# An attention stage on one core: the global keys' product cut into four 64x64 tiles, and the copy of the transposed weights shared by two engines

## The chip, the core and the metric

The kernel runs on one core of a Trainium2 chip. The metric is the device time of one execution in microseconds; lower is better. A core has five engines that each take their own instructions in order: PE (TensorE, matrix products and transposes), DVE (VectorE), ACT (ScalarE), POOL (GpSimd) and SP (SyncE, which issues most DMAs). Engines wait for each other through semaphores. PE writes its results to PSUM, eight banks of 128 partitions by 512 float32; the other engines copy them from there to SBUF.

## The reference, cut to what matters

Attention over 4 x 8 heads with 512 local tokens and 32 global tokens of 64 numbers, followed by two dense blocks on the result (the second and third part of the kernel; the change does not touch them).

```python
s_ll = scale * q_l @ k_l.T; s_ll = where(|pos_i - pos_j| <= 32, s_ll, -1e9)
s_lg = scale * q_l @ k_g.T
a_l = softmax(concat([s_lg, s_ll]))
out_l = a_l @ concat([v_g, v_l])
s_g = scale * q_g @ concat([k_g, k_l]).T
out_g = softmax(s_g) @ concat([v_g, v_l])
x = concat([out_g, out_l])
```

A local query thus has two products with values: with the 32 global values, which all queries share, and with the values of its own window.

## The kernel before, in words

**Tiles and units.** `body` works on one pair of heads at a time: `p` runs over 16 pairs (`NP`). A pair's 512 queries are cut in two halves `u`, each of 256 queries, which are four windows of 64 queries. One (p, u) is the unit of the stage; a pass of the loop over `p` (line 930) holds two units' worth of every step, and "half A" below is its first, "half B" its second.

**Steps of a unit.** `scores` (lines 732 to 740) makes the products of queries and keys as 64x64 tiles: eight matrix products of 160 columns into two PSUM banks `s`; float32 takes two passes, so 16 instructions. `maxima` (742) is DVE's: per 128x160 tile it adds the mask, writes the sum to SBUF and takes the maximum. `exps` (751) is ACT's, with the sums as a by-product. `sums` and `norm` (758, 761) make the reciprocal on DVE and scale the four tiles on POOL. `transp` (779) transposes them on PE into bank `tc0` (four 128x128, the window keys) and `tc1` (one 128x128, the global keys). `transp_evac` (786) copies both to SBUF: ACT the 128x512 of `tc0` (line 788, to `p1`), DVE the 128x128 of `tc1` (line 790, to `p2`). `pv` (792) makes the products with the values: `glob` (806, two products of 128x128 weights with the 128 columns of `p2`) and `win` (799, eight products of 128x64 weights with 96 or 64 columns). Unit u writes PSUM bank `pv_ps[u]`. `pv_local` (825) and `pv_global` (831) copy that bank to `x` on DVE.

**Order.** The schedule is written by hand: each engine gets its instructions in the order of the loop body. In a pass p, PE does `scores(p,0)`, `transp(p-1,0)`, `pv(p-2,1)`, on odd p the global queries' scores `g_scores` (853), `scores(p,1)`, on even p the global queries' transposes `g_transp` (882), `transp(p-1,1)`, `pv(p-1,0)`. DVE does the maxima of (p,0), the reciprocal of (p-1,1), `pv_global(p-2,0)`, the `p2` copy of (p-1,0), on odd p three operations on the global queries (856 to 862), the maxima of (p,1), `pv_local` and `pv_global` of (p-2,1), the `p2` copy of (p-1,1). ACT does per half: two `exps`, the 128x512 copy, two `exps`; on even p two copies of `g_transp` (885, 886) stand ahead of the copy of half B.

**Other work in the same loop.** In passes 10 to 13 DVE has at the end of half B one 128x512 subtraction each (`x_low`, 216). In passes 8, 14, 16 and 17 it converts pieces of weights (`w_float`, 155, in three steps `step(0)` to `step(2)`, and a cast, 180). Passes 16 and 17 have no scores: `mm1` (224) of the first dense block stands in their place.

Of the kernel before, what the change touches and what calls it, by code (L numbers as in the profile page):

```python
# [22 lines left out]
DM, DFF = 512, 2048  # L23
# [58 lines left out]
def body(ctx, tc, qT, kW, v, w1i, w1o, w2i, w2o, coef, out):  # L82
# [50 lines left out]
    pv_ps = [ps.tile([128, 512], F32, name=f"pv{j}") for j in range(2)]  # L133
# [573 lines left out]
    p1_r = Ring("p1", ATT2 + 2 * VC + 2560, 640, 3, 2, 320)  # L707
# [24 lines left out]
    def scores(p, u):  # L732
        for i in range(2):
            for j in range(2):
                for a in range(2):
                    r, w = slice(64 * j, 64 * j + 64), 4 * u + 2 * i + (a if i else 1 - a)
# [35 lines left out]
    def g_copies(p, u):  # L772
        p1 = pT[p, u][0]
        a = pgT[p // 2][0]
        o = 64 * (p % 2)
        pool.tensor_copy(p1[:, :, 128:192].rearrange("p j (s c) -> p j s c", s=2),
                         a[:, 2 * u:2 * u + 2, o:o + 64].rearrange("p s (j c) -> p j s c", j=2))
# [14 lines left out]
    def pv(p, u):  # L792

        v = vt[p // 2]
        c = pgT[p // 2][1]
        p1, p2 = pT.pop((p, u))
        bank = pv_ps[u]

        def win(w, o0, o1, stop=False):
            for j in range(2):  # L800
                jj = 2 * (p % 2) + j
                pe.matmul(bank[64 * j:64 * j + 64, o0:o1], v[:, VW * w + 64 * jj:VW * w + 64 * jj + 64],  # L802
                          p1[:, j, o0 + (32 if o0 >= 128 else 0):o1 + (32 if o0 >= 128 else 0)],
                          start=False, stop=stop, skip_group_check=True)
# [7 lines left out]
        glob(0)  # L812
        glob(1)
        win(4 * u, 64, 160)
        win(4 * u + 1, 0, 64)
        win(4 * u + 2, 128, 224)
        win(4 * u + 3, 224, 288, stop=u == 0)
        if u:
            for j in range(2):
                jj = 2 * (p % 2) + j  # L820
                o = VE + 64 * jj
                pe.matmul(bank[64 * j:64 * j + 64, 128:160], v[:, o:o + 64], c[:, 32 * jj:32 * jj + 32],
                          start=False, stop=True, skip_group_check=True)

    def pv_local(p, half):
# [665 lines left out]
```

## Time and profile before

| | us |
|---|---|
| three runs | 843.36, 843.52, 844.43 |
| median | 843.52 |
| profiled execution, first to last instruction (span) | 841.8 |
| attention loop in the profile, first scores to the first product of pass 17 | 4.4 to 114.7 |
| PE busy over the span | 831.1 (99%) |
| DVE, ACT, POOL busy over the span | 707.4, 620.1, 187.2 |

The page gives no time for the profiled execution other than its span; the median of the runs is 1.7 us above the span, which is what lies around the instructions. TensorE's granted clock is at its upper level in all 40 slices of the page, and no run stands out. In the timeline view a row is one instruction or several alike that follow each other: start in us from the span's start, time it took, engine, line, operation, tiles, count, and in brackets idle time of the engine ahead of it. The time that an instruction took includes its way through the engine, so the next may start before it ends; what an instruction costs its engine is the distance from its start to the next start.

### The profile page before, as it was taken

What the parts mean: (1) busy time and instruction counts of PE and PEld (TensorE: products, weight loads), DVE (VectorE), ACT (ScalarE), POOL (GpSimd) and SP (SyncE); (2) the same over time, 40 slices, a digit from 0 to 9 for tenths busy, and PEclk for the clock granted to TensorE, in tenths of its full rate; (3) what the DMA queues carried; (4) which work ended last, traced back from release to release, by engine and by line L of the source; (5) the groups of instructions that cost most, each with busy time, mean ns of one, the idle gap of its engine ahead of it and who ended that gap; (6) DMA issues with size and microseconds to landing.
All of it is one profiled execution on the core that took longest, in us unless ns stands there. A gap on an engine that the chain in (4) does not pass through costs nothing.

```text
span 841.8 us, 15593 instructions
## 1 busy us (share of the span) xinstructions
PE 831.1 (99%) x5719; PEld 761.9 (91%) x5719; DVE 707.4 (84%) x1411; ACT 620.1 (74%) x1195; POOL 187.2 (22%) x352
## 2 busy tenths in 40 slices
PE   8999999999999999999999999999999999999997
PEld 4877788889999999999999999999899999898986
DVE  5687888994893597877968699999999999989997
ACT  6888867773453666767776797878897878888775
POOL 4666765660001111111111121111011011011100
PEclk9999999999999999999999999999999999999999
DMA  9686759922768899989987573433463443465401
GB/s 342 253 315 238 272 200 418 406 78 100 278 231 289 278 326 390 330 280 370 383 283 225 149 240 112 126 113 113 125 188 113 125 113 113 125 207 146 138 25 63
DMA packets 50540, 181.37 MB, mean 215 GB/s; under 512 B 5664, under 2 KB 8480, under 8 KB 49440
## 3 DMA queue, kind: packets, MB, share of 16 engines
q1 hardware_dynamic: 30976, 100.94, 32.0%
q0 software_dynamic: 18960, 79.18, 31.1%
q8 instruction: 45, 0.74, 0.4%
q10 hardware_dynamic: 528, 0.26, 0.1%
q14 instruction: 31, 0.25, 0.1%
HBM read 139.73 MB, written 40.63 MB: 214 GB/s over the span
## 4 chain that ended last, share of the span: by engine, by line
PE 84%; DVE 11%; ACT 2%; POOL 2%; issue 1%; ACTq 0%; POOLq 0%
PE s L404 27%; PE s L431 10%; PE pv L431 10%; PE tc L431 10%; PE s L233 9%; PE tc L243 5%; PE pv L243 5%; PE pv L802 2%; PE tc L783 2%; POOL sm L766 2%; PE s L738 1%; PE pv L808 1%; DVE g L496 1%; DVE x L516 1%; DVE x L520 1%; DVE e L512 1%
## 5 line engine op out<-in xcount | busy, mean ns | idle before, releaser
L404 PE MATMUL s<-sh,got 128*128 128x320 f32 (+1 forms) x1120 | 287.8, 320 | 0.8 <-DVE x L592 0.6
L404 PEld LDWEIGHTS s<-sh,got 128*128 128x128 f32 x1120 | 198.6, 188 | 2.9 <-DVE x L592 1.0
L396 POOL DMA_DIRECT2D got<-pr x120 | 64.7, 539 | 539.8 <-PE s L404 464.6
L404 PE MATMUL s<-sl,got 128*128 128x320 f32 (+1 forms) x560 | 179.1, 320 | 0.0
L431 PEld LDWEIGHTS s<-g,w 128*128 128x128 f32 x768 | 124.7, 188 | 10.9
L431 PE MATMUL s<-g,w 128*128 128x256 f32 x768 | 131.7, 280 | 0.0
L404 PEld LDWEIGHTS s<-sl,got 128*128 128x128 f32 x560 | 105.4, 188 | 0.9
L431 PE MATMUL tc<-g,w 128*128 128x384 f32 (+1 forms) x384 | 99.3, 366 | 0.2 <-DVE g L496 0.2
L431 PE MATMUL pv<-g,w 128*128 128x384 f32 (+1 forms) x384 | 99.1, 366 | 0.0
L233 PE MATMUL s<-xh,w 128*128 128x512 f32 (+1 forms) x256 | 76.8, 363 | 0.0
L492 ACT ACTIVATE g<-x 128x640 fp32r<-128x640 f32 (+1 forms) x79 | 61.4, 777 | 14.8 <-DVE x L537 13.1
L496 DVE TENSOR_TENSOR g<-x,g 128x640 fp32r<-128x640 f32 (+1 forms) x79 | 69.0, 874 | 1.0 <-ACT g L492 0.9
L431 PEld LDWEIGHTS tc<-g,w 128*128 128x128 f32 x384 | 65.2, 188 | 3.5 <-DVE g L496 0.8
L431 PEld LDWEIGHTS pv<-g,w 128*128 128x128 f32 x384 | 65.1, 188 | 2.8
L755 ACT ACTIVATE sm<-sm,nm 128x160 f32<-128x160 f32 x128 | 55.6, 441 | 9.3 <-DVE nm L747 9.0
L766 POOL TENSOR_SCALAR sm<-sm,rs 128x160 f32<-128x160 f32 x128 | 54.2, 449 | 34.3 <-DVE x L836 16.1
L512 DVE SCALAR_TENSOR_TENSOR e<-e,nf,e 128x768 f32<-128x768 f32 (+1 forms) x48 | 46.6, 971 | 10.4 <-ACT e L504 10.4
L233 PEld LDWEIGHTS s<-xh,w 128*128 128x128 f32 x256 | 47.3, 188 | 5.1
L747 DVE CUSTOM_DVE_ANT_0 sm<-s,mask 128x160 f32<-128x160 f32 x128 | 36.2, 321 | 15.7 <-PE s L738 8.9
L188 POOL TENSOR_TENSOR w<-cv,w 128x512 fp32r<-128x512 f32 x32 | 42.1, 1318 | 30.9 <-ACT w L182 23.1
L617 ACT ACTIVATE u<-s 128x320 f32<-128x320 f32 (+1 forms) x40 | 18.3, 457 | 41.4 <-PE s L404 41.4
L508 ACT ACTIVATE x<-x,nf 128x768 f32<-128x768 f32 (+1 forms) x48 | 47.1, 981 | 0.0
(192 smaller groups left out, 1748.3 us busy)
## 6 DMA issues: line engine op xcount, KB each, us to landing
got<-pr POOLq DMA_DIRECT2D x80, 512.0 KB, 4.1
got<-pr POOLq DMA_DIRECT2D x40, 768.0 KB, 4.8
pr<-half SPq DMA_DIRECT2D x24, 512.0 KB, 6.9
v<-in_v_dram SPq DMA_DIRECT2D x8, 1408.0 KB, 8.2
k<-in_kW_dram SPq DMA_DIRECT2D x15, 592.0 KB, 5.8
r<-in_w1i_dram SPq DMA_DIRECT2D x16, 512.0 KB, 9.8
r<-in_w1o_dram SPq DMA_DIRECT2D x16, 512.0 KB, 10.6
pr<-tw SPq DMA_DIRECT2D x16, 512.0 KB, 3.2
```

What stands on the lines that cost most here:

```text
L188: pool.tensor_tensor(w[:, 1], f, w[:, 0].bitcast(F32), op=ALU.subtract)
L233: pe.matmul(ph, w[:, half, 128 * kk:128 * kk + 128], b[:, kk, :n], start=(half == kk == 0 and b is hi), stop=(half == 1 and kk == KD - 1))
L243: pe.matmul(acc_bank[d][:, :n], w[:, half, 128 * d:128 * d + 128], src[:, :n], start=start, stop=stop)
L396: pool.dma_start(got[q % 2][:, o0:o1], pairs[q >= Q2][q % NPAIR][:, o0:o1])
L404: pe.matmul(bank(q, i), a[:, k], b[:, k], start=first and k == 0 and j == 0, stop=k == 1 and j == 2, skip_group_check=True)
L431: pe.matmul(dst, a, b, start=first and j == 0, stop=j == KF - 1 and final, skip_group_check=True)
L492: act.activation(gpair(q, f)[0], strip(q, 2 + f), AF.Copy)
L496: eng.tensor_tensor(gl, strip(q, 2 + f), gh.bitcast(F32), op=ALU.subtract)
L508: act.activation(t, h, AF.Identity, scale=nf[:, 3:4], bias=nf[:, 2:3])
L512: dve.scalar_tensor_tensor(a, in0=a, scalar=nf[:, 5:6], in1=b, op0=ALU.mult, op1=ALU.add)
L755: act.activation(e, e, AF.Exp, scale=-1.0, bias=nm[:, k:k + 1], accum_out=tot[:, k:k + 1])
L766: pool.tensor_scalar(e, e, rs[:, k:k + 1], 1.0, op0=ALU.mult, op1=ALU.mult)
```

## The change

The 128x128 products with the global values become four products of 64x64 weights (`common`), which write two banks: the first two windows of a unit go with bank 0 and the other two with bank 1, for both units, so that one bank now holds columns of both units and `pv_local` and `pv_global` read both banks. `pv` is split into `windows` and `common`, and `common` stands directly ahead of the next `scores` on PE. The copy of `tc0` is halved: ACT copies the first head's 256 columns, DVE the second's. `pv_local(p-2,0)` moves ahead of the maxima of (p,0), `pv_local(p-2,1)` and both parts of `pv_global` ahead of the maxima of (p,1). The order of the windows in the output and the layout of `p1` follow.

```diff
-    pv_ps = [ps.tile([128, 512], F32, name=f"pv{j}") for j in range(2)]
+    pv_two = ps.tile([128, 1024], F32, name="pv")
+    pv_ps = [pv_two[:, 512 * j:512 * j + 512] for j in range(2)]
...
     def transp_evac(p, u):
         p1, p2 = pT[p, u]
-        act.copy(bass.AP(tensor=p1.tensor, offset=p1.offset, ap=[p1.ap[0], [320, 2], [192, 2], [1, 128]]),
-                 tc_ps[0].rearrange("p (a b c) -> p a b c", a=2, b=2))
+        o = 32 if u else 0
+        for j, copy in enumerate((act.copy, dve.tensor_copy)):
+            copy(p1[:, j, :, o:o + 128], tc_ps[0][:, 256 * j:256 * j + 256].rearrange("p (i c) -> p i c", i=2))
         dve.tensor_copy(p2, tc_ps[1][:, 0:128])
...
-        def glob(i):
-            o = VG + 256 * (p % 2) + 128 * i
-            pe.matmul(bank[:, 160 * i:160 * i + 128], v[:, o:o + 128], p2, start=i == 0, stop=False,
-                      skip_group_check=True)
...
+    def windows(p, u):
+        v, p1 = vt[p // 2], pT[p, u][0]
+        for i in range(2):
+            w = 4 * u + 2 * i
+            for w, o, c, n in ((w, 0, 128, 96), (w + 1, 96, 224, 64)) if u else ((w, 64, 64, 96), (w + 1, 0, 0, 64)):
+                for j in range(2):
+                    jj = 2 * (p % 2) + j
+                    pe.matmul(pv_ps[i][64 * j:64 * j + 64, c:c + n], v[:, VW * w + 64 * jj:VW * w + 64 * jj + 64],
+                              p1[:, j, i, o:o + n], start=u == w % 2 == 0, stop=False, skip_group_check=True)
...
+    def common(p, u):
+        v, p2 = vt[p // 2], pT.pop((p, u))[1]
+        for i in range(2):
+            for j in range(2):
+                r, o = slice(64 * i, 64 * i + 64), VG + 256 * (p % 2) + 128 * i + 64 * j
+                pe.matmul(pv_ps[i][64 * j:64 * j + 64, 160 * u:160 * u + 128], v[r, o:o + 64], p2[r],
+                          start=False, stop=True, skip_group_check=True, tile_position=(64 * i, 64 * j))
...
                 scores(p, 0)
-                maxima(p, 0, 0)
-                exps(p, 0, 0)
             else:
                 mm1(p - NP)
             if 2 <= p:
                 pv_local(p - 2, 0)
+            if cur:
+                maxima(p, 0, 0)
+                exps(p, 0, 0)
...
             if 2 <= p:
-                pv(p - 2, 1)
+                windows(p - 2, 1)
             if odd and p > 1:
                 g_scores(g)
+            if 2 <= p:
+                common(p - 2, 1)
             if cur:
...
+            if 2 <= p:
+                pv_local(p - 2, 1)
+                pv_global(p - 2)
+            if cur:
                 maxima(p, 1, 0)
...
-            if 2 <= p:
-                pv_local(p - 2, 1)
-                pv_global(p - 2, 1)
             if pre:
                 transp(p - 1, 1)
...
             if pre:
-                pv(p - 1, 0)
+                windows(p - 1, 0)
+                common(p - 1, 0)
```

How the instructions stand on the engines, in the order of each engine; names in brackets are the semaphores that the instruction waits for, numbers behind names are buffers (`sm` the score tiles, `p_1` and the like `p1` and `p2`, `tc_182` is `tc0`).

DVE before, half A of a pass with even p, from the reciprocal of (p-1,1) to the first maximum of (p,1):

```order
L763 RECIPROCAL rs_417<-rs_417 128x4 [waits DVE_49]
L836 COPY x_62<-pv_184 128x32
L790 COPY p_1_403<-tc_183 128x128 [waits PE_49]
L747 ISA sm_425,nm_407<-s_180,mask_402 128x160 [waits PE_49,Pool_49]
```

The same place now:

```order
L764 RECIPROCAL rs_416<-rs_416 128x4 [waits DVE_49]
L791 COPY p_1_427<-tc_182 128x2x128 [waits Activation_49]
L792 COPY p_1_402<-tc_183 128x128 [waits PE_49]
L821 COPY x_62<-pv 128x256 [waits PE_49]
L827 COPY x_62<-pv 128x32
L828 TENSOR_TENSOR x_62<-x_62,pv 128x32 [waits DVE_49]
L748 ISA sm_424,nm_406<-s_180,mask_401 128x160 [waits PE_49,Pool_49]
```

Between the reciprocal and the maximum, DVE now has its half of the `tc0` copy, which waits for ACT, and the copies of the values' products of (p-2,1), which stood behind the maxima before.

PE before, from the transposes of a half B to the next scores:

```order
L783 MATMUL tc_182<-ident_401,sm_425 128x128 [waits Activation_49,Pool_49]
L783 MATMUL tc_182<-ident_401,sm_425 128x128 [waits Pool_49] x3
L784 MATMUL tc_183<-ident_401,sm_425 128x128 [waits DVE_49]
L808 MATMUL pv_184<-p_2_404,v_423 128x128 [waits DMAHW6_49]
L808 MATMUL pv_184<-p_2_404,v_423 128x128
L802 MATMUL pv_184<-p_2_429,v_423 64x96 [waits Pool_49]
L802 MATMUL pv_184<-p_2_429,v_423 64x96
L802 MATMUL pv_184<-p_2_429,v_423 64x64 x2
L802 MATMUL pv_184<-p_2_429,v_423 64x96 x2
L802 MATMUL pv_184<-p_2_429,v_423 64x64 x2
L738 MATMUL s_178<-k_435,q_431 64x160 [waits Activation_49]
```

The same place now:

```order
L784 MATMUL tc_182<-ident_400,sm_424 128x128 [waits DVE_49,Pool_49]
L784 MATMUL tc_182<-ident_400,sm_424 128x128 [waits Pool_49] x3
L785 MATMUL tc_183<-ident_400,sm_424 128x128 [waits DVE_49]
L801 MATMUL pv<-p_2_428,v_422 64x96 [waits DMAHW6_49,DVE_49,Pool_49]
L801 MATMUL pv<-p_2_428,v_422 64x96
L801 MATMUL pv<-p_2_428,v_422 64x64 x2
L801 MATMUL pv<-p_2_428,v_422 64x96 x2
L801 MATMUL pv<-p_2_428,v_422 64x64 x2
L815 MATMUL pv<-p_2_403,v_422 64x128 x4
L739 MATMUL s_178<-k_434,q_430 64x160 [waits Activation_49]
```

The two 128x128 products are gone from behind the transposes and four 64x64 ones stand ahead of the scores; the transposes wait for DVE where they waited for ACT, and the windows wait for DVE as well, since the banks that they write hold the other unit's columns.

DVE before, at the end of pass 10, with that pass's `x_low`:

```order
L829 COPY x_62<-pv_185 128x256
L838 TENSOR_TENSOR x_62<-x_62,pv_185 128x32
L790 COPY p_2_404<-tc_183 128x128 [waits PE_49]
L219 TENSOR_TENSOR xl_101<-x_62,xh_100 128x512
L747 ISA sm_426,nm_408<-s_178,mask_402 128x160 [waits PE_49,Activation_49,Pool_49]
```

The same place now:

```order
L791 COPY p_2_428<-tc_182 128x2x128 [waits Activation_49]
L792 COPY p_2_403<-tc_183 128x128 [waits PE_49]
L220 TENSOR_TENSOR xl_101<-x_62,xh_100 128x512
L821 COPY x_62<-pv 128x256 [waits PE_49]
L748 ISA sm_425,nm_407<-s_178,mask_401 128x160 [waits PE_49,Pool_49]
```

`x_low` stands where it stood, between the `p2` copy and the next pass's first maximum, and now has the wait for ACT ahead of it and the copy of the values' product behind it.

## Rows read from the trace of the kernel before

**Rows 1.** Windows view, two passes: length, then PE, PEld, DVE, ACT, POOL busy (instructions):

```profile
37.35:49.92 12.57, 12.32 (x189) 10.07 (x185) 9.09 (x57) 10.62 (x43) 7.87 (x22) 1.00 0.65 238
```

**Rows 2.** Timeline of PE, one half with its groups:

```profile
75.65 0.77 PE L738 MATMUL s<-k,q 64*64 64x160 f32 x16
76.36 0.74 PE L783 MATMUL tc<-ident,sm 128*128 128x128 f32 x4
...
77.05 0.61 PE L808 MATMUL pv<-p,v 128*128 128x128 f32 x4
77.59 0.78 PE L802 MATMUL pv<-p,v 128*64 128x96 f32 x16
```

**Rows 3.** Timeline of DVE, then ACT: from a maximum to ACT's copy:

```profile
105.74 0.33 DVE L747 CUSTOM_DVE_ANT_0 sm<-s,mask 128x160 f32<-128x160 f32 x1 [0.88 <-PE s L738]
...
107.22 0.42 DVE L829 COPY x<-pv 128x256 f32<-128x256 f32 x1
...
106.11 0.45 ACT L755 ACTIVATE sm<-sm,nm 128x160 f32<-128x160 f32 x1 [0.42 <-DVE nm L747]
...
106.98 0.56 ACT L788 COPY p<-tc 128x512 f32<-128x512 f32 x1
```

**Rows 4.** Groups by line and form, 200 us to the end: count, busy us, mean ns:

```profile
L446 ACT ACTIVATE x<-s 128x256 f32<-128x256 f32 x16 | 5.8, 382 | 0.7 <-PE s L431 0.5
```

**Rows 5.** Timeline of DVE, end of pass 13, with `x_low`:

```profile
94.88 0.41 DVE L829 COPY x<-pv 128x256 f32<-128x256 f32 x1
95.20 0.18 DVE L838 TENSOR_TENSOR x<-x,pv 128x32 f32<-128x32 f32 x1
95.30 0.29 DVE L790 COPY p<-tc 128x128 f32<-128x128 f32 x1
95.50 0.89 DVE L219 TENSOR_TENSOR xl<-x,xh 128x512 fp32r<-128x512 f32 x1
96.31 0.31 DVE L747 CUSTOM_DVE_ANT_0 sm<-s,mask 128x160 f32<-128x160 f32 x1
```

**Rows 6.** Timeline, odd pass: DVE and ACT around the global scores; even pass: ACT's copies:

```profile
41.13 0.66 DVE L856 TENSOR_REDUCE gm<-s 128x1 f32<-128x480 f32 x1 [0.98 <-PE s L853]
...
42.09 0.32 DVE L747 CUSTOM_DVE_ANT_0 sm<-s,mask 128x160 f32<-128x160 f32 x1
...
43.21 0.44 ACT L755 ACTIVATE sm<-sm,nm 128x160 f32<-128x160 f32 x1
...
48.92 0.58 ACT L885 COPY pg<-s 128x512 f32<-128x512 f32 x1
...
49.55 0.60 ACT L788 COPY p<-tc 128x512 f32<-128x512 f32 x1
```

**Rows 7.** Timeline of DVE, pass 14: the weights' three steps:

```profile
97.77 0.39 DVE L164 TENSOR_SCALAR cv<-cv 128x512 int32<-128x512 int32 x1
...
98.20 0.78 DVE L166 SCALAR_TENSOR_TENSOR cv<-r,cv 128x512 int32<-128x512 int32 x1
...
99.10 0.69 DVE L171 SCALAR_TENSOR_TENSOR cv<-r,cv 128x512 int32<-128x512 int32 x1
```

**Rows 8.** Timeline of PE: where passes 3, 14 and 16 begin:

```profile
24.81 0.37 PE L738 MATMUL s<-k,q 64*64 64x160 f32 x4
...
94.70 0.37 PE L738 MATMUL s<-k,q 64*64 64x160 f32 x4
...
107.95 0.50 PE L233 MATMUL s<-xh,w 128*128 128x512 f32 x1
```

**Rows 9.** Timeline of DVE, then PE, in pass 16:

```profile
111.81 1.39 DVE L171 SCALAR_TENSOR_TENSOR cv<-r,cv 128x512 int32<-128x512 int32 x2
113.12 0.84 DVE L180 CAST w<-cv 128x512 fp32r<-128x512 f32 x2
...
113.98 0.78 PE L802 MATMUL pv<-p,v 128*64 128x96 f32 x16
114.69 0.50 PE L233 MATMUL s<-xh,w 128*128 128x512 f32 x1
```

More of the change, by code (lines that the diff above doesn't have):

```diff
@@ L706, in body @@
     sm_r = Ring("sm", ATT2 + 2 * VC, 640, 4, 2 * KW, 2)
-    p1_r = Ring("p1", ATT2 + 2 * VC + 2560, 640, 3, 2, 320)
+    p1_r = Ring("p1", ATT2 + 2 * VC + 2560, 640, 3, 2, 2, KW)
     q_r = Ring("q", END - 4 * (QC + KC), QC, 4, QC)
@@ L735, in scores @@
                 for a in range(2):
-                    r, w = slice(64 * j, 64 * j + 64), 4 * u + 2 * i + (a if i else 1 - a)
+                    r, w = slice(64 * j, 64 * j + 64), 4 * u + 2 * i + (a if u else 1 - a)
                     c = window(w) - 32 * i
@@ L774, in g_copies @@
         a = pgT[p // 2][0]
-        o = 64 * (p % 2)
-        pool.tensor_copy(p1[:, :, 128:192].rearrange("p j (s c) -> p j s c", s=2),
+        o, c = 64 * (p % 2), 0 if u else 128
+        pool.tensor_copy(p1[:, :, :, c:c + 32],
                          a[:, 2 * u:2 * u + 2, o:o + 64].rearrange("p s (j c) -> p j s c", j=2))
@@ L821, in pv, with pv_local, pv_global @@
                 o = VE + 64 * jj
-                pe.matmul(bank[64 * j:64 * j + 64, 128:160], v[:, o:o + 64], c[:, 32 * jj:32 * jj + 32],
-                          start=False, stop=True, skip_group_check=True)
-    def pv_local(p, half):
+                pe.matmul(pv_ps[0][64 * j:64 * j + 64, 128:160], v[:, o:o + 64], pgT[p // 2][1][:, 32 * jj:32 * jj + 32],
+                          start=False, stop=False, skip_group_check=True)
+    def common(p, u):
[5 more added lines that the diff above has]
+                          start=False, stop=True, skip_group_check=True, tile_position=(64 * i, 64 * j))
+    def pv_local(p, u):
         b, hp = divmod(p, 4)
-        o = pv_ps[half][:, 0:320].rearrange("p (a b) -> p a b", a=2)[:, :, 0:128]
-        dst = x[:, hp, SL * b + 256 * half:SL * b + 256 * half + 256]
-        dve.tensor_copy(dst.rearrange("p (a b) -> p a b", a=2), o)
-    def pv_global(p, half):
+        dst = x[:, hp, SL * b + 256 * u:SL * b + 256 * u + 256]
+        dve.tensor_copy(dst.rearrange("p (a b) -> p a b", a=2),
+                        pv_two.rearrange("p (a b) -> p a b", a=2)[:, :, 160 * u:160 * u + 128])
+    def pv_global(p):
         b, hp = divmod(p, 4)
-        o = pv_ps[half][:, 128:160]
         dst = x[:, hp, B * SL + SG * b:B * SL + SG * b + SG]
-        if half == 0:
-            dve.tensor_copy(dst, o)
-        else:
-            dve.tensor_tensor(dst, dst, o, op=ALU.add)
+        dve.tensor_copy(dst, pv_ps[0][:, 128:160])
+        dve.tensor_tensor(dst, dst, pv_ps[1][:, 128:160], op=ALU.add)
     def g_scores(g):
@@ L971, in body @@
             step(0)
-            if 2 <= p:
-                pv_global(p - 2, 0)
             step(1)
```

20 lines of the change are left out of this document (1 added, 19 removed).

## The prediction

> **What bounds the kernel now.** I read the windows view first, for two passes of the attention loop without work on weights [rows 1]. PE is busy for 12.32 of 12.57 us, ACT for 10.62, DVE for 9.09, POOL for 7.87; the reader is to see that PE has no room and DVE the most after POOL. Then the timeline of PE, where the distance from one group's start to the next is what the group costs [rows 2]: scores 0.71, transposes 0.69 (76.36 to 77.05), the two 128x128 products with the global values 0.54 (77.05 to 77.59). The groups stand back to back, so the loop goes at PE's pace. The last two views are the timelines of DVE and ACT, for what each operation costs and how long DVE's results take to come back from ACT [rows 3, 5, 6, 7]. DVE's 9.09 us hide behind PE because none of its operations waits for ACT's copy of the transposes. That is what the change touches.
>
> "0.2%" below is 1.7 us, about what a measurement of this kernel can tell from no change. Durations are of the one profiled execution, span 841.8 us; the sum is a difference to it and is added to the median, 843.52, which lies 1.7 above the span.
>
> **The change part by part.** *The global product on PE.* Out go 0.54 us per unit [rows 2], 32 units. In come eight 64x64 instructions of 128 columns. No row has them; the nearest is the scores' group, sixteen 64x64 instructions of 160 columns in 0.71, so half the instructions and four fifths of the columns: 0.28. Bounds: four at a time at 0.12 each (0.69 / 5 transposes of 128 columns [rows 2]) is 0.24, one after another 8 x 0.12 = 0.96. I take 0.28, since the scores are the same shape of tile. The change of shape between transposes and windows, some 0.1 of the 0.54 (four instructions at 0.11 are 0.44), stays. PE is relieved by 0.16 per half, up to 0.25 if the scores start faster behind tiles of their own shape; I take 0.2. That is 0.8 of 12.56 per two passes: PE alone could do them in 11.8.
>
> *The halved copy.* ACT's 128x512 (0.56 [rows 3]) becomes 128x256. The nearest row is ACT's own 128x256 out of PSUM, 0.38 [rows 4]; bounds 0.28 (half of 0.56) and 0.56. DVE gets the other 128x256: its copy of that size from PSUM takes 0.42 in all [rows 3] and lets the next start after 0.32 [rows 5]; I take 0.35, hand-over included, bounds 0.2 (the 128x128, 95.30 to 95.50) and 0.42. The listing of DVE's order says more than the diff: DVE's half waits for ACT. It names the engine only, but ACT has no other instruction here that touches this tile or this buffer than its own half; and the transposes, which must wait until both halves are out, now wait for DVE alone. So the halves go one after the other, and DVE, which takes its instructions in order, stands still until ACT is through. ACT in turn has two exponentials ahead of its copy, and these wait for DVE's maxima. DVE waits for ACT and ACT for DVE, once each per half: a ring.
>
> The Trainium skill (TensorEngine Tiling (Array Packing), Performance Considerations) says that a faster TensorE leaves the PSUM copies as the likely bound, and to use both ScalarE and VectorE for them. By that advice the two halves run side by side and the change is a gain on both engines, the first rival below; by the order, sharing the copy ties the two engines together, which is the forecast.
>
> *The ring's length* is counted from the first maximum of one half to the first of the next. From the maximum to the start of ACT's copy it is 1.24 (105.74 to 106.98 [rows 3]); ACT's half 0.38, DVE's half 0.35 and the `p2` copy 0.20 [rows 4, 5] make 2.17. In half A of an even pass follow `pv_local(p-2,1)`, 0.32, now ahead of the maxima, and the two 128x32 of `pv_global`, 0.18 (the second waits for the first) and 0.10 [rows 5]: 2.77. Half A of an odd pass has the global reductions, 0.96 (41.13 to 42.09 [rows 6]), besides: 3.73. Half B of an odd pass has `pv_local(p-1,0)`, 0.32, and 0.15 because ACT has the global exponentials first (it reached the next ones 1.12 after the maximum, 42.09 to 43.21 [rows 6]; the maximum now comes 0.60 later, and 0.37 is usual, 105.74 to 106.11 [rows 3]): 2.64. Half B of an even pass has the 0.32 as well, and ACT's two global copies ahead of its half, 0.63 (48.92 to 49.55 [rows 6]): 3.12.
>
> An odd pass is 6.37, an even one 5.89, together 12.26: longer than PE's 11.8, a little shorter than the 12.57 of before. DVE's other operations ahead of its half cost nothing while they fit in the wait: between the maximum and the copy it has 1.48 us of them (105.74 to 107.22 [rows 3]), ACT's half ends at 1.62. What stands behind the half is in the ring in full.
>
> *The sum.* Passes 3 to 13 took 69.89 (24.81 to 94.70 [rows 8]). Now: passes 3, 5, 7, 9 four times 6.37, passes 4 and 6 twice 5.89, together 37.26. Pass 8 has weights' steps: 0.43 and 0.70 ahead of DVE's half (97.77 to 98.20, and 98.20 to 99.10 less the 0.20 of `p2` [rows 7]), of which about 0.5 fit in the wait, and 0.66 behind it (1.31 for two [rows 9]): 5.89 + 1.29 = 7.18. Passes 10 to 13: 24.52 and four `x_low` at 0.81 (95.50 to 96.31 [rows 5]), which was mostly covered by DVE's spare time and now stands in the ring: 27.76. Sum 72.20: **2.3 longer**.
> Passes 14 and 15 took 13.25 (94.70 to 107.95 [rows 8]); now 7.18, and 5.3 for pass 15, behind which no maximum waits (half A 2.77, half B at PE's pace, an estimate of 2.5 from [rows 2]): 0.75 shorter. Pass 16: DVE's half must wait for ACT's (about 112.0) and ends with `p2` at 112.5; then two weights' steps 1.31, `pv_local` and `pv_global` 0.60 to 114.45. Only then may the windows of (15,0) start, since both units share both banks; before they started at 113.98 and `mm1` at 114.69 [rows 9]. Windows 0.71, four tiles 0.28: 115.45, **0.8 later**. Pass 17: 0.2 shorter. The start: the four tiles stand ahead of the scores of pass 2, with nothing else on PE's path shorter there, 0.3 later.
> 2.3 - 0.75 + 0.8 - 0.2 + 0.3 = 2.5. Behind the loop everything follows PE, which is as busy as before. **Forecast 846.0**, 0.3% slower.
>
> The moves of `pv_local` ahead of the maxima cost nothing by themselves where scores are late, as before; that cover is gone in the ring, and their 0.32 and 0.28 are in the sum. POOL's queue is not passed by anything; its one copy per unit has the same size. SP's queue is as it was.
>
> **The rivals.**
> *PE goes on setting the pace.* The hand-over is covered, because ACT gets to its half early enough. For it: DVE's own load would be 9.09 + 4 x 0.35 = 10.5 of 11.8, and ACT's falls; both fit. Against it: the order of waits above. It decides where the ring of two passes falls under 11.8, that is 0.12 per half less than worked out, with `x_low` and pass 16 absorbed too. Then 32 x 0.2 = 6.4 faster: **837**, the other side of the forecast.
> *A shorter ring.* The ring exists, but each half is 0.12 shorter (ACT's half at its lower bound of 0.28 would do). The plain passes then gain with PE, `x_low` and pass 16 still cost: 22 halves less 0.12 is 2.6 off the forecast, **843.4**, no change.
> *The four tiles do not overlap.* At 0.96 a unit PE has 0.68 more than taken: 3.14 - 0.2 + 0.68 = 3.6 per half, where it had 3.14 (12.57 / 4), in some 28 halves: 13 slower, **856**. Against it: sixteen 64x64 scores take 0.71 where one after another would take 2.
>
> **How the numbers follow.** The ring as worked out 0.6, its own range 844 to 850: ACT's copy between 0.28 and 0.56 and DVE's between 0.2 and 0.42 move a half by -0.25 to +0.25 at the far ends, and by 0.1 either way, 2 us in all, near the rows taken. PE's pace 0.16, the shorter ring 0.2, tiles that don't overlap 0.04. The range 837 to 850 takes in the first fully and the others but the last and about half of the second. Faster: PE's pace and a quarter of the shorter ring, 0.21. Same: the rest of the shorter ring and the low end of the forecast (to 845.2), 0.22. Slower: 0.57.
>
> **What would show it.** DVE's 128x256 copy out of `tc` should start within 0.1 us of the end of ACT's and be DVE's longest wait; the stretch from a first maximum to the next should be near 2.8 and 3.1 in even passes, 3.7 and 2.6 in odd ones; PE should wait for DVE at transposes or windows; passes 10 to 13 should be 0.8 longer than their neighbours, and `mm1` of pass 17 should wait behind the windows. The prediction is wrong if two passes take 11.8 us with PE back to back (first rival), if DVE's half starts without waiting for ACT, or if the four tiles take more than 0.4 us.

## The result, and the profile after

| | before | after |
|---|---|---|
| median of four runs on one chip, us | 843.68 (843.36 to 844.43) | 850.20 (848.82 to 851.49) |
| ratio, 95% interval | | 1.0075 (1.0063 to 1.0087) |
| profiled execution: its own time, span | span 841.77 | 849.01, span 847.24 |

0.75% slower: beyond the 0.2% that a measurement can tell, in the direction of the forecast, and 4 us more than it (846.0); the median lies 0.2 us above the end of the range. Between the two profiled executions the difference is 5.47 us, and that is what the views can divide; the medians are 6.5 apart, so the profiled run of the change is one of its faster ones, and some 1.0 of the median is in no profile.

**The loop.** First the windows view of after, over two passes without weights' work, with the columns of [rows 1]:

```profile
37.50:49.90 12.40, 11.90 (x209) 9.19 (x205) 10.76 (x62) 9.88 (x43) 7.89 (x22) 1.00 0.69 261
```

Against [rows 1] PE is busy 0.4 less, ACT 0.7 less, DVE 1.7 more, and the two passes are 0.17 shorter. The plain passes are not where the time went. Two lines of the view of waits for the same stretch (engine, tile and line, what it waited for, us in total, times, longest):

```profile
DVE p L791 <- ACT p L791: 2.1, 4, 0.7
ACT sm L756 <- DVE nm L748: 1.6, 3, 0.7
```

DVE waits for ACT and ACT for DVE, as forecast. (The stretch cuts a half: one of DVE's four waits, 0.7, lies ahead of it. Two whole passes hold three, 1.4 in all, none in half B of the odd pass, where DVE is busy until ACT is through.) One half in full, from the timelines of DVE and then ACT (start, time, engine, line, operation):

```profile
44.81 0.32 DVE L748 CUSTOM_DVE_ANT_0 sm<-s,mask 128x160 f32<-128x160 f32 x1
...
46.42 0.42 DVE L791 COPY p<-tc 128x256 f32<-128x256 f32 x1 [0.25 <-ACT p L791]
46.77 0.28 DVE L792 COPY p<-tc 128x128 f32<-128x128 f32 x1
46.96 0.41 DVE L821 COPY x<-pv 128x256 f32<-128x256 f32 x1
...
47.63 0.33 DVE L748 CUSTOM_DVE_ANT_0 sm<-s,mask 128x160 f32<-128x160 f32 x1
```
```profile
45.17 0.45 ACT L756 ACTIVATE sm<-sm,nm 128x160 f32<-128x160 f32 x1 [0.41 <-DVE nm L748]
...
46.05 0.34 ACT L791 COPY p<-tc 128x256 f32<-128x256 f32 x1
46.30 0.45 ACT L756 ACTIVATE sm<-sm,nm 128x160 f32<-128x160 f32 x1
```

The first maximum starts at 44.81, ACT's first exponential behind it at 45.17, ACT's half of the copy at 46.05 to 46.39, DVE's half 0.03 later, and the next first maximum at 47.63: the half A of an even pass is 2.82, forecast 2.77.

On PE the four tiles cost what was taken. Its timeline:

```profile
45.18 0.27 PE L785 MATMUL tc<-ident,sm 128*128 128x128 f32 x1
45.39 0.78 PE L801 MATMUL pv<-p,v 128*64 128x96 f32 x16
46.00 0.26 PE L807 MATMUL pv<-pl,v 128*64 128x32 f32 x4
46.19 0.45 PE L815 MATMUL pv<-p,v 64*64 64x128 f32 x8
46.46 0.72 PE L739 MATMUL s<-k,q 64*64 64x160 f32 x16
47.11 0.66 PE L871 MATMUL s<-ident,gs 128*128 128x128 f32 x4
```

`common` takes 0.27 (46.19 to 46.46; forecast 0.28, against 0.54 in [rows 2]), and the scores behind it 0.65 instead of 0.71.

**Where the 5.47 arose.** PE's starts of the same places, in the timeline of after (passes 3, 14, 16, 17, and the product of `mm1` behind the loop), and the last one of before, whose others are in [rows 8, 9]:

```profile
24.62 0.92 PE L739 MATMUL s<-k,q 64*64 64x160 f32 x16
...
96.25 0.72 PE L739 MATMUL s<-k,q 64*64 64x160 f32 x16
...
110.53 0.50 PE L234 MATMUL s<-xh,w 128*128 128x512 f32 x1
...
118.18 0.50 PE L234 MATMUL s<-xh,w 128*128 128x512 f32 x1
...
122.31 0.50 PE L234 MATMUL s<-xh,w 128*128 128x512 f32 x1
```
```profile
118.88 0.50 PE L233 MATMUL s<-xh,w 128*128 128x512 f32 x1
```

| stretch | before | after | longer by | forecast |
|---|---|---|---|---|
| up to pass 3 | 24.81 | 24.62 | -0.19 | +0.3 |
| passes 3 to 13 | 69.89 | 71.63 | +1.74 | +2.3 |
| passes 14 and 15 | 13.25 | 14.28 | +1.03 | -0.75 |
| pass 16 | 6.74 | 7.65 | +0.91 | +0.8 |
| pass 17 | 4.19 | 4.13 | -0.06 | -0.2 |
| the rest, to the end of the span | 722.89 | 724.93 | +2.04 | 0 |

Two entries are far off: passes 14 and 15, and the rest. Part of the first belongs to passes 3 to 13, as is worked out further down.

**The end.** The last products of before and of after on PE, from their timelines:

```profile
835.37 0.39 PE L431 MATMUL tc<-w,g 128*128 128x512 f32 x1
835.60 0.84 PE L431 MATMUL pv<-w,g 128*128 128x512 f32 x3
...
836.96 0.39 PE L431 MATMUL s<-w,g 128*128 128x512 f32 x1
```
```profile
839.00 0.40 PE L432 MATMUL tc<-w,g 128*128 128x512 f32 x1
839.25 0.40 PE L432 MATMUL pv<-w,g 128*128 128x512 f32 x1
840.33 0.73 PE L432 MATMUL pv<-w,g 128*128 128x512 f32 x2 [0.69 <-ACT x L462]
...
841.59 0.40 PE L432 MATMUL s<-w,g 128*128 128x512 f32 x1
```

Before, three products into `pv` follow each other: the first is the last into bank `pv0`, the other two go to bank `pv1`. After, these two wait 0.69 for ACT's copy out of bank `pv0`:

```profile
839.68 0.60 ACT L462 ACTIVATE x<-pv 128x512 f32<-128x512 f32 x1 [0.22 <-PE pv L432]
```

The banks are two, but the change made them one tile (`pv_two`), and the program orders all that touches one tile. It does so for DVE's copy out of `pv1` too, which the listing now has waiting for ACT's copy out of `pv0`. With that the last two output transfers stand in the listing the other way round, ACT's last. SP waits at the end for each transfer in a fixed order of semaphores; ACT's transfer, the last to land, now has one that is waited for early, so that SP's other checks follow behind it, 0.8 in all, where they lay under it before. SP's longest waits at the end, before and after:

```profile
SPq L1482 <- DMA out_dram<-x: 1.7, 1, 1.7
```
```profile
SPq L1474 <- DMA out_dram<-x: 2.5, 1, 2.5
```

From the product ahead of the wait to the last one it is 1.36 before (835.60 to 836.96) and 2.34 after (839.25 to 841.59): 0.98. From the last one to the end of the span it is 4.81 before (836.96 to 841.77) and 5.65 after (841.59 to 847.24): 0.84. Together 1.82 of the 2.04. What is left arises between 379 and 400 us, around the first copies out of the same banks (the function `leave`): the same products of PE come 3.45 later ahead of that stretch and 3.72 later behind it.

### The profile page after: what moved, and what is told of

It reads as the page before. It is cut to its first block, busy times and chain, and to the rows that moved or that the text cites. A ratio compares the mean times of both kernels' runs of the same rounds, so it can differ in the third digit from the quotient of the medians.

```text
span 847.2 us, 15893 instructions
## 1 busy us (share of the span) xinstructions
PE 828.6 (98%) x5847; PEld 754.2 (89%) x5847; DVE 721.8 (85%) x1443; ACT 614.7 (73%) x1195; POOL 186.1 (22%) x352
## 4 chain that ended last, share of the span: by engine, by line
PE 82%; DVE 13%; ACT 2%; POOL 1%; issue 1%; POOLq 0%; ACTq 0%
PE s L405 27%; PE s L432 10%; PE pv L432 10%; PE tc L432 10%; PE s L234 9%; PE tc L244 5%; PE pv L244 5%; PE pv L801 2%; PE tc L784 2%; PE s L739 1%; DVE g L497 1%; POOL sm L767 1%; DVE x L517 1%; DVE x L521 1%; DVE e L513 1%
## 5 line engine op out<-in xcount | busy, mean ns | idle before, releaser
L521 DVE SCALAR_TENSOR_TENSOR x<-x,nf 128x768 f32<-128x768 f32 (+1 forms) x48 | 46.5, 970 | 0.4
```

Source lines behind the costliest of these rows:

```text
L521: dve.scalar_tensor_tensor(t, in0=t, scalar=nf[:, 1:2], in1=h, op0=ALU.add, op1=ALU.mult)
```

## The experiments

All times are medians; before was measured again beside each group of runs and lay between 843.4 and 844.1. "Two passes" is the time from the first maximum of pass 5 to that of pass 7 unless another pair is named, "behind the loop" that from the third `mm1` to the end of the span.

| kernel | us | ratio to before (95%) | two passes | third `mm1` | behind the loop |
|---|---|---|---|---|---|
| before | 843.4 to 844.1 | | 12.56 | 118.88 | 722.9 |
| the change | 850.2 | 1.0075 (1.0063 to 1.0087) | 12.44 | 122.31 | 724.9 |
| whole copy on ACT | 845.85 | 1.0026 (1.0015 to 1.0037) | 12.03 | 119.03 | 725.1 |
| halves alone | 846.38 | 1.0030 (1.0019 to 1.0042) | 12.81 | 121.16 | 723.1 |
| halves from two tiles | 847.11 | 1.0040 (1.0027 to 1.0052) | 12.02 | 120.47 | 726.0 |
| own pv tiles | 848.45 | 1.0054 (1.0039 to 1.0069) | 12.54 | 123.09 | 724.4 |
| whole copy, own pv tiles | 843.87 | 1.0005 (0.9995 to 1.0014) | 12.18 | 119.14 | 722.8 |
| the change again | 849.87 | 1.0076 (1.0060 to 1.0092) | 12.42 | 122.34 | 725.5 |

**The halving undone.**

```diff
-        for j, copy in enumerate((act.copy, dve.tensor_copy)):
-            copy(p1[:, j, :, o:o + 128], tc_ps[0][:, 256 * j:256 * j + 256]...)
+        act.copy(p1[:, :, :, o:o + 128], tc_ps[0].rearrange("p (j i c) -> p j i c", j=2, i=2))
```

> The change with one part undone: ACT copies the whole 128x512 of the transposes again; the four 64x64 tiles in two banks, their order and the shared pv tile stay. Ring theory (DVE's half waits for ACT's half, ACT for DVE's maxima): without the hand-over PE sets the pace, two plain passes take 11.8 us instead of about 12.6, the attention loop ends (third mm1) near 115 instead of 122.3; the shared pv tile still costs about 1.8 us at the very end; total 839.5 (838 to 842). Rival (the two shared banks make PE wait for both evacuations, the halving is harmless): loop end stays near 122, total 849 to 851.

Measured 845.85, 4.3 below the change (850.20), and 0.26% above before. So the halving costs more than anything else in the change; the rival, for which it is harmless, falls. But the expectation of 839.5 falls as well: two passes take 12.03, not 11.8, and the loop is no shorter than before's at its end (119.03 to 118.88). The four tiles give back less than PE's groups promise even without the ring.

**The halving alone**, in the kernel before (two 128x128 products, a bank per unit):

```diff
-        act.copy(bass.AP(tensor=p1.tensor, offset=p1.offset, ap=[p1.ap[0], [320, 2], [192, 2], [1, 128]]), tc_ps[0]...)
+        for j, copy in enumerate((act.copy, dve.tensor_copy)):
+            copy(bass.AP(tensor=p1.tensor, offset=p1.offset + 320 * j, ap=[p1.ap[0], [192, 2], [1, 128]]),
+                 tc_ps[0][:, 256 * j:256 * j + 256]...)
```

> The kernel before with the halving alone: ACT copies half of the transposes, DVE the other half; the global product stays two 128x128 matmuls, one bank per unit, the order as before. Ring theory: the longest of PE's pace (3.14 a half) and the ring sets the half, not their sum; with pv_local between maxima and copy the ring is about 2.2 to 2.6 in plain halves, under PE's 3.14, and longer only in the halves with global reductions, weights' steps or x_low: 843.5 to 847, likeliest 845, loop end near 120. Rival (a half copied by DVE after ACT costs 0.2 or more in every half, whatever else runs): 850 or more, loop end 125.

Measured 846.38, where 843.5 to 847 was expected; the loop is 2.3 longer, the rest as before. DVE's wait for ACT is there (0.5 in two passes, the row below, from the view of waits), and smaller than the 1.4 of the change: here `pv_local` stands between the maxima and the copy, so that DVE has something to do meanwhile.

```profile
DVE p L789 <- ACT p L789: 0.5, 2, 0.3
```

The halving by itself is thus a loss of 0.3%.

**The halves from two PSUM tiles.** The second head's transposes go to bank `tc1`, behind the 128 columns of `p2`:

```diff
-            pe.transpose(tc_ps[0][:, 128 * k:128 * k + 128], s[:, o:o + 128, k // 2], ident)
+            c = 128 * (k % 2) + 128 * (k // 2)
+            pe.transpose(tc_ps[k // 2][:, c:c + 128], s[:, o:o + 128, k // 2], ident)
...
-            copy(..., tc_ps[0][:, 256 * j:256 * j + 256]...)
+            copy(..., tc_ps[j][:, 128 * j:128 * j + 256]...)
```

> The change with the second half of the transposes put in the other bank, behind the 128 columns of p2, so that ACT reads tc0 alone and DVE tc1 alone; everything else stays. If DVE waits because two engines read one PSUM tile, the wait is gone, the ring is cut and PE sets the pace: loop end near 115, total 839.5 (838 to 842, the shared pv tile still costing about 1.8 at the end). Rival 1 (the wait comes from the shared SBUF buffer that both write): DVE's half still starts at the end of ACT's, total 849 to 851. Rival 2 (DVE's added work sets the pace by itself, 10.5 us and more of two passes): DVE busy without waits, total 843 to 848.

The wait is gone. DVE's half and ACT's half run side by side, from the timelines of DVE and ACT at the place shown above:

```profile
46.06 0.39 DVE L792 COPY p<-tc 128x256 f32<-128x256 f32 x1
```
```profile
45.99 0.35 ACT L792 COPY p<-tc 128x256 f32<-128x256 f32 x1
```

That settles where the wait came from: the shared PSUM tile, not the shared buffer `p1`, which both still write. (Each of these tiles is one bank, so this run does not tell tile from bank.) The Trainium skill (PSUM — Partial Sum Buffer, "PSUM bank collisions raise a hardware error") says that two engines must not touch the same bank and quadrant (32 partitions) at once, reads included, so that the compiler orders them; the 0.03 between the end of ACT's half and the start of DVE's agrees. It would not ask for the wait at the end, which lies between two banks. The total is 847.11, not 839.5. The shared pv tile still costs its part behind the loop (726.0, of which 1.0 is a wait for a weight, below), and with two passes at 12.02 the loop still ends 1.6 late: in passes 11 and 13 half B takes 3.40 where the kernel with the whole copy takes 2.78, since DVE has its half and `x_low`. There the second rival, DVE's own work, is right.

**Two pv tiles.**

```diff
-    pv_two = ps.tile([128, 1024], F32, name="pv")
-    pv_ps = [pv_two[:, 512 * j:512 * j + 512] for j in range(2)]
+    pv_ps = [ps.tile([128, 512], F32, name=f"pv{j}") for j in range(2)]
...
-        dve.tensor_copy(dst.rearrange("p (a b) -> p a b", a=2),
-                        pv_two.rearrange("p (a b) -> p a b", a=2)[:, :, 160 * u:160 * u + 128])
+        for i in range(2):
+            dve.tensor_copy(dst[:, 128 * i:128 * i + 128], pv_ps[i][:, 160 * u:160 * u + 128])
```

> The change with the two pv banks as two tiles again, and pv_local therefore as two 128x128 copies; the halves stay. Theory on the end: the last strip's matmul into bank pv1 waits 0.69 us for ACT's copy out of pv0 only because both banks are one tile, and the swapped order of the last two output transfers costs 0.8 more; with two tiles the time from the third mm1 to the end of the span is that of before, 722.9, instead of 724.9. The ring stays and grows by 0.08 a half (two copies of 0.20 instead of one of 0.32): loop end near 124.5, total 849 to 851. Rival (the 2 us behind the loop come from the weights' transfers that the later loop pushes): 724.9 or more behind the loop, total 852.

Measured 848.45, 0.6 below what was expected: the loop ends at 123.09 and not near 124.5. The end is that of before: in PE's timeline three products into `pv` follow each other again, and from the last product it is 4.81 to the end of the span (842.68 to 847.49).

```profile
841.29 0.86 PE L431 MATMUL pv<-w,g 128*128 128x512 f32 x3
...
842.68 0.39 PE L431 MATMUL s<-w,g 128*128 128x512 f32 x1
```

Yet behind the loop it is 724.4 and not 722.9: 1.3 of it are lost between 323 and 335 us, at a wait that has nothing to do with the tiles. PE's wait, ACT's timeline there, and ACT's in the change:

```profile
PE s L404 <- ACT u L556: 0.7, 1, 0.7
```
```profile
329.85 0.68 ACT L152 ACTIVATE cw<-raw 128x512 f32<-128x512 f32 x1 [1.69 <-DMA raw<-in_w2i_dram]
```
```profile
327.06 0.69 ACT L153 ACTIVATE cw<-raw 128x512 f32<-128x512 f32 x1 [0.60 <-DMA raw<-in_w2i_dram]
```

ACT converts a weight when its transfer lands; here it stood 1.69 for it, in the change 0.60, and PE stood behind ACT. Of the sixteen profiles of this study ten show this wait, with 0.2 to 1.3 us of PE's time each, and it does not go by how late the loop ends; why it comes in some and not in others is not shown.

**Both undone**: whole copy, two pv tiles.

> Two parts of the change undone: ACT copies the whole 128x512 again, and the pv banks are two tiles again (pv_local is two 128x128 copies). Left are the four 64x64 tiles, two banks, and pv_local ahead of the maxima. Theory (the shared pv tile costs 1.8 us at the very end, the ring the rest): as the run with the whole copy less 1.8, 844.0 (843 to 845), the end of the span 720.1 behind mm1 of pass 18 if no transfer is late; DVE has room for the 0.08 a half. Rival (what remains of the loss is not the shared tile): 845.9.

Measured 843.87, 2.0 below the whole copy alone and the same as before (1.0005). So the change divides, one part undone after the other: 4.3 for the halving, 2.0 for the shared tile, nothing for the four tiles with their two banks and moved copies, which were not taken apart. These parts are not without effect: from PE's start of pass 3 to that of pass 14 it is 68.94 in this kernel (24.92 to 93.86), 0.95 less than before, and passes 14 to 17 give it back.

**The change once more.**

> The change itself once more. 848.8 to 851.5. Its first runs lay at 848.9 and at 851.4; theory: the stretch 300 to 400 us has the DMA engines busy for 0.99 of the time, ACT converts a weight there when its transfer lands and PE waits behind ACT by 0 to 1.3 us, so a run at the upper value shows PE waits there of 1 to 2 us more than the first profile; the rest of the profile repeats within 0.2 us. Rival: the two values differ inside the attention loop, by 2 us at the third mm1.

849.04 to 851.18 over its runs; the profile differs from the first by 0.63 in all, nearly all of it the wait for the weight at 333 us, and by 0.03 at the third `mm1`. The rival is out for this run; but none of the profiles is of a run near 851.4, so what those have more is not shown.

**The copies moved back behind the maxima**, on the kernel with both undone: `pv_local` and `pv_global` stand where the kernel before had them.

```diff
-            if 2 <= p:
-                pv_local(p - 2, 0)
             if cur:
                 maxima(p, 0, 0)
                 exps(p, 0, 0)
+            if 2 <= p:
+                pv_local(p - 2, 0)
...
-            if 2 <= p:
-                pv_local(p - 2, 1)
-                pv_global(p - 2)
             if cur:
                 maxima(p, 1, 0)
...
                 maxima(p, 1, 1)
+            if 2 <= p:
+                pv_local(p - 2, 1)
+                pv_global(p - 2)
```

> As the run with the whole copy and two pv tiles, and pv_local and pv_global behind the maxima as in the kernel before. Theory (ahead of the maxima they make the first maximum wait for the four tiles that stand just ahead of the scores: DVE waited 0.9 us in two plain passes for them, and the scores of the next half wait in turn): two passes go from 12.1 to 11.8, and the total is 842 (840.5 to 843.5). Rival (both units share both banks, so the next windows wait for the later copy out of them): windows wait for DVE's pv_local in most halves, two passes 12.3 or more, total 845 or more.

858.16, 1.0173 (1.0156 to 1.0189): my expectation had the wrong sign, the rival was right and more so. Passes 3 and 4 take 14.46 together. DVE's timeline in pass 9, and PE's windows there:

```profile
77.50 0.48 DVE L820 COPY x<-pv 128x128 f32<-128x128 f32 x2
77.90 0.18 DVE L825 COPY x<-pv 128x32 f32<-128x32 f32 x1
```
```profile
78.18 0.78 PE L799 MATMUL pv<-p,v 128*64 128x96 f32 x16 [1.35 <-POOL sm L766]
```

The windows start 0.1 behind the end of `pv_global`'s first copy (78.08). The row names POOL as what came last, but the listing has the windows waiting for DVE's copies out of these banks too. Both units write both banks, so a copy that comes later holds the next unit's windows. The early copies are the price of the two banks, not a free move.

**The same with the halves from two tiles.**

> As the run before this one, but with the halved copy, each engine on its own PSUM tile (tc0 for ACT, tc1 for DVE), so without the ring. ACT is relieved by 0.2 a half, DVE loaded by 0.3. Theory (DVE's work, not a wait, now sets the halves with x_low, weights' steps and global reductions): plain passes as fast as or faster than with the whole copy, passes 10 to 13 slower by 0.5 in their second half, total 843.5 (842 to 846). Rival (relieving ACT is what the loop wants): 841 or less.

859.42, 1.0190 (1.0174 to 1.0206), passes 3 and 4 again 14.46 together: neither the expectation nor its rival came true; the copies out of the banks set the pace, whoever copies the transposes. Passes 3 and 4 are taken here because TensorE's granted clock fell later in both profiles, to its lower level (1.2 GHz) for 3.4 us: from 48.0 to 51.4 in the first, with PE busy for 7.0 of the 10 us ahead of it, and from 70.8 to 74.2 in the second, with PE busy for 7.3 of 10.8. In the first, passes 5 and 6 take 15.97, so that some 1.5 of the 14.3 by which it exceeds the kernel with both undone go with the lower clock. In the other fourteen profiles the clock stays at its upper level from 8 us to PE's last product.

**The tiles ahead of the global queries.** In odd passes `common`, `pv_local` and `pv_global` go ahead of `g_scores`, on the kernel with both undone; then with `pv_global` alone behind two maxima; then with the halves from two tiles.

```diff
-            if odd and p > 1:
-                g_scores(g)
             if 2 <= p:
                 common(p - 2, 1)
+                pv_local(p - 2, 1)
+                pv_global(p - 2)
+            if odd and p > 1:
+                g_scores(g)
...
-            if 2 <= p:
-                pv_local(p - 2, 1)
-                pv_global(p - 2)
```

> As the run with the whole copy and two pv tiles (843.9), and in odd passes the four 64x64 tiles, pv_local and pv_global go ahead of the products and reductions of the global queries instead of behind them. Theory (in the odd half A DVE stood idle for 1.0 us until the global products were there, and took pv_local and pv_global, 0.67, only behind the reductions, so that the maxima of the next half came that much later): the odd half A goes from 4.2 to about 3.8, seven odd passes give 2.5, the extra change of tile shape on PE takes 0.1 each back: 841.5 (840.5 to 842.5), faster than the kernel before. Rival (PE sets the pace there, DVE's order is free): 843.9 and PE without a wait.

> As the run before this one, with pv_global alone behind the first two maxima. If DVE's chain into the maxima still sets the half, another 0.2 in some halves, 840 to 841.5; if the windows of the other unit, which write the banks that pv_global reads, wait for it, no gain or a loss of up to 0.2 a half (841.5 to 846).

> The order of the first run of this call with the halved copy, ACT on tc0 and DVE on tc1. Theory (cut free of the ring, DVE has too much work in the passes with x_low and weights' steps, ACT's relief helps in plain passes): 842 to 844, passes 11 and 13 in half B 3.4 instead of 2.8. Rival (DVE has room enough in this order): 841 or less.

844.05 (1.0003, 0.9994 to 1.0012), 844.21 (1.0008, 0.9999 to 1.0017) and 844.15 (1.0004, 0.9995 to 1.0013): none differs from before. The gain that was expected of the first did not come, the second took its branch without a gain, and the third lies 0.15 above its range, with 3.17 and not 3.4 in half B of passes 11 and 13. In the first, half A of pass 5 went from 4.14 to 3.92 as meant, and half A of pass 6 from 2.89 to 3.13: two passes 12.26. (Its loop ends 0.7 earlier than with both undone, 118.45, and its profile has 1.3 of the wait for the weight.) What was gained in one half was waited for in the next, so something else sets two passes.

**Half of the normalisation left out**, on the kernel with both undone.

```diff
-        for k in range(4):
+        for k in range(2):
             e = s[:, KW * (k % 2):KW * (k % 2) + KW, k // 2]
             pool.tensor_scalar(e, e, rs[:, k:k + 1], 1.0, op0=ALU.mult, op1=ALU.mult)
```

> As the run with the whole copy and two pv tiles, but POOL multiplies only two of the four blocks of exponentials of a half by the reciprocal sums; the other two stay unnormalised, so the output leaves that part out. Theory (with the four tiles PE's own groups make 11.7 us of two passes, and the half microsecond above it is PE waiting at the transposes for POOL's last blocks): two plain passes 11.7 to 11.8 instead of 12.1 to 12.2, loop 3 us shorter, total 841 (839.5 to 842). Rival (the loop is held by PE itself, or by DVE's pv_local that waits for the tiles): two passes stay at 12.1, total 843.5 or more.

839.64, 0.9952 (0.9935 to 0.9968), two passes 11.73, as the theory said; the loop ends 4.5 earlier than with both undone (114.66). The transposes of the same half on PE's timeline, with both undone and then with half the normalisation:

```profile
44.16 1.17 PE L783 MATMUL tc<-ident,sm 128*128 128x128 f32 x4 [0.26 <-POOL sm L766]
45.16 0.27 PE L784 MATMUL tc<-ident,sm 128*128 128x128 f32 x1
```
```profile
42.95 0.71 PE L783 MATMUL tc<-ident,sm 128*128 128x128 f32 x4 [0.26 <-POOL sm L766]
43.50 0.27 PE L784 MATMUL tc<-ident,sm 128*128 128x128 f32 x1
```

Four transposes take 1.00 where they wait for POOL block by block, 0.55 where two of the blocks are there. A busy share hides this: the long group counts as work of PE.

**One block of four to DVE**, the computation complete; then the same with the tiles ahead.

```diff
-            pool.tensor_scalar(e, e, rs[:, k:k + 1], 1.0, op0=ALU.mult, op1=ALU.mult)
+            (pool if k else dve).tensor_scalar(e, e, rs[:, k:k + 1], 1.0, op0=ALU.mult, op1=ALU.mult)
```

> As the run with the whole copy and two pv tiles, with one of the four blocks of a half normalised by DVE right behind the reciprocals, the other three by POOL, so the output is complete. Theory (PE waits at the transposes for POOL's last block): POOL's blocks take 0.38 each, so the last is ready 0.38 earlier; DVE gets some 0.25 a half, 1.0 of two passes on 9.96, under PE's 11.7. Half A of an even pass goes from 2.9 to 2.6, two passes to 11.8, total 842 (840.5 to 843). Rival (DVE is as near to its limit as POOL, its extra work delays the maxima by as much): 843.5 to 845.

> The same with the four tiles, pv_local and pv_global ahead of the global products in odd passes. There the odd half A was 0.2 shorter and the halves behind it longer by as much, since POOL's blocks came no earlier; with POOL relieved both gains should add: total 841 (839.5 to 842.5). Rival (PE's own groups, 11.7, with one more change of tile shape, are reached already in the run before this one): the same as that run, within 0.5.

842.91 (0.9992, 0.9983 to 1.0001) and 844.03 (1.0004, 0.9995 to 1.0013). In the first, half A of pass 6 falls from 2.89 to 2.38, two passes to 11.89, and the third `mm1` comes at 117.20, 1.7 ahead of before; the wait confirms itself in a complete kernel. But 1.2 of that are given back at 323 us, where ACT stands 1.61 for a weight and PE behind it:

```profile
323.80 0.67 ACT L152 ACTIVATE cw<-raw 128x512 f32<-128x512 f32 x1 [1.61 <-DMA raw<-in_w2i_dram]
```

It is the fastest complete kernel of the study, and its lead over the kernel before is within what can be told from none. The second one's expectation, that both gains add, is a miss: two passes are 12.15.

## Why the prediction was wrong

**Right: the ring and its parts.** The listing's wait became the longest wait of DVE, its half started 0.03 behind ACT's (forecast: within 0.1), and the halves took 2.82, 3.91, 3.13 and 2.57 (passes 6 and 7) against 2.77, 3.73, 3.12 and 2.64. From the start of ACT's half to that of DVE's it is 0.37 (46.05 to 46.42; 0.38 in the sum), DVE's cost 0.35 as taken. Two passes were 12.4 (forecast 12.26), the difference being half A of the odd pass. `x_low` in the ring in full: half B of pass 10 went from 3.17 to 3.73, half B of pass 11 from 3.04 to 3.40, and from the neighbours of after (3.13 and 2.57) these are 0.60 and 0.83, forecast 0.81; without the ring, with the whole copy on ACT, both are 2.9 or less. Pass 16 waited for `pv_global` as worked out, 0.91 for 0.8; DVE's copies and then PE's windows in the timelines of after:

```profile
116.21 0.42 DVE L821 COPY x<-pv 128x256 f32<-128x256 f32 x1
...
116.76 0.19 DVE L828 TENSOR_TENSOR x<-x,pv 128x32 f32<-128x32 f32 x1
```
```profile
117.09 0.78 PE L801 MATMUL pv<-p,v 128*64 128x96 f32 x16 [0.99 <-DVE x L828]
```

**The step that failed: "Behind the loop everything follows PE, which is as busy as before."** PE is as busy, but the order that the program imposes there is not the same: the merged pv tile ties products and copies of two banks together. That costs a wait of 0.69 on PE and 0.84 in the order of the last transfers, and the stretch behind the loop is 2.04 longer in all, where the sum has 0. The prediction read the merged tile for the loop alone, and priced no place outside it where these banks are used. The runs settle it: the product's wait of 0.69, and 5.6 from PE's last product to the end, stand in all four profiles with the shared tile (the change twice, the whole copy, the halves from two tiles), and neither in the twelve with two tiles, which have 4.8.

**A term that was off: "5.3 for pass 15", with "half B at PE's pace, an estimate of 2.5".** Between PE's starts passes 14 and 15 were 1.03 longer instead of 0.75 shorter, a miss of 1.8. But 1.0 of it is a matter of where it was counted. The sum adds up lengths from first maximum to first maximum and sets them against distances between PE's starts, and the two drift apart. The first maxima of passes 3, 14 and 15 in DVE's timeline of after, and PE's starts:

```profile
25.90 0.32 DVE L748 CUSTOM_DVE_ANT_0 sm<-s,mask 128x160 f32<-128x160 f32 x1
...
98.49 0.31 DVE L748 CUSTOM_DVE_ANT_0 sm<-s,mask 128x160 f32<-128x160 f32 x1
...
105.74 0.32 DVE L748 CUSTOM_DVE_ANT_0 sm<-s,mask 128x160 f32<-128x160 f32 x1
```
```profile
104.46 0.92 PE L739 MATMUL s<-k,q 64*64 64x160 f32 x16 [0.47 <-ACT pg L874]
...
107.27 0.72 PE L739 MATMUL s<-k,q 64*64 64x160 f32 x16
107.93 1.47 PE L784 MATMUL tc<-ident,sm 128*128 128x128 f32 x4
109.23 0.27 PE L785 MATMUL tc<-ident,sm 128*128 128x128 f32 x1
```

The scores of pass 3 start 1.28 ahead of the first maximum (24.62 to 25.90). Those of pass 14 start 2.24 ahead (96.25 to 98.49): PE has run on while `x_low` kept DVE busy. Those of pass 15 wait for ACT's copies of the global transposes, and it is 1.28 again (104.46 to 105.74). From maximum to maximum passes 3 to 13 took 72.59, where the sum has 72.20, and pass 14 took 7.25, where it has 7.18. So the ring was right there within 0.5, a little too short, and the 0.6 by which passes 3 to 13 seem shorter than forecast is not a gain. What is left is pass 15, 6.07 (104.46 to 110.53) for 5.3, and that is its half B: half A took 2.81 (forecast 2.77), half B 3.26 (107.27 to 110.53). Its pace is not PE's. The four transposes of (14,1) take 1.30 (107.93 to 109.23), where four take 0.55 when two of the blocks are there (the run with half the normalisation); POOL's blocks already held them before, at 1.06, and the forecast had them follow PE.

Of the 3.0 by which the profiled difference exceeds the forecast, 2.0 thus arise behind the loop, 0.8 in half B of pass 15, 0.5 in the ring of passes 3 to 14 and 0.2 in passes 16 and 17; the start, 0.5 better than forecast, hid part of it by luck.

**The rivals.** "PE goes on setting the pace", 837, was worked out as what is left when the ring is gone; with the ring gone the kernel takes 843.9 to 847, because two passes are 12.0 to 12.2: POOL's blocks come between. PE's own 11.8 was right (11.73 with half the normalisation). The advice of the Trainium skill that the prediction weighed (TensorEngine Tiling (Array Packing), Performance Considerations), to give the copies to both engines, holds here with a tile for each: then they run side by side, from 45.99 and 46.06. It did not make this kernel faster, since DVE had no room for its half in the passes with `x_low`. "The four tiles do not overlap" is out: 0.27 a group. (The working of its bounds has a slip, 0.69 / 5 is 0.14 and not 0.12, which would put them at 0.28 and 1.1; the forecast does not use them.) The other thing said to cost nothing, "the moves of `pv_local` ahead of the maxima", is true only against an alternative that is worse: left behind the maxima, on the kernel with both undone, they cost 14, of which some 1.5 go with the lower clock in the profiled run.

**Still open:** why the eight runs of the change spread from 848.8 to 851.5, three of them above 851; the wait for a weight near 330 us accounts for 0.6 in the one pair of profiles.

## What to carry to other kernels

Before a PSUM tile is shared, look for every place in the program that uses its banks, and for every two engines that read it: the program orders what touches one tile, and a wait can turn up hundreds of microseconds away, or close a ring between two engines that both had room. Sharing a copy between two engines wants two tiles in two banks, and an engine with room for its half in the fullest pass, not in the mean one. And a pace read from groups that stand back to back is an upper bound on what a faster group gives: look at which engine's results arrive block by block inside a long group.

## What was not expected of the hardware

A group of four 64x64 tiles with 128 columns, eight instructions, takes 0.27 from its start to that of the next group of the same tile shape; from the last 128x128 transpose to the 128x64 windows pass 0.21 in after (45.18 to 45.39), 0.1 more than from it to the 128x128 products before (0.11, 76.94 to 77.05). That 0.1 only moved: before, it stood between those products and the windows. Whether the change of shape as such causes it is not shown: the single 128x64 transpose of the global queries stands between 128x128 ones with 0.11 on either side (47.60 in after).

The final checks cost by their order: with the same five output transfers, the same 256 KB in the last one and the same 2.9 us to its landing, 4.8 or 5.6 pass from PE's last product to the end, by which transfer is checked first.
